# Batch 0's output matmuls regrouped inside cycles 6 to 8: one 64x64 run per cycle

## The chip, the cores and the metric

The kernel runs on one core of a Trainium2 chip. The metric is the device time of one execution in microseconds (us). Three runs of the kernel before gave 340.65, 340.74 and 341.85 us, median 340.74. A core has a matrix engine (TensorE, PE in the profile; its weight loads are PEld), a vector engine (DVE), an activation engine (ACT), GpSimd (POOL) and SyncE (SP). Here POOL issues the loads and SP issues the transposing DMAs and the stores. Each engine works through its own list of instructions in order and waits on semaphores that the others raise.

## The reference

`reference()` is sigmoid attention followed by an MLP-mixer block, on q, k, v of shape (8, 12, 448, 64):

```python
scores = np.matmul(q, k.transpose(0, 1, 3, 2)) / np.sqrt(64) - np.log(448)
attn_out = np.matmul(1.0 / (1.0 + np.exp(-scores)), v)          # (8, 12, 448, 64)
x = attn_out.transpose(0, 2, 1, 3).reshape(8, 448, 768)
h = np.maximum(x.transpose(0, 2, 1) @ w_tok1, 0.0) @ w_tok2       # tokens 448 -> 256 -> 448
u = x + h.transpose(0, 2, 1)
h2 = np.maximum(u @ w_ch1, 0.0) @ w_ch2                           # channels 768 -> 1536 -> 768
return u + h2
```

## The kernel before

The twelve heads of a batch are handled as three units of four heads, so there are 8 x 3 = 24 cycles, numbered c = 3b + u (b the batch, u the unit). A cycle has seven score steps. `qk(b, u, j)` (L187) makes a group of four 64x64 matmuls, which use the four quarters of the matrix engine at once and together stream 448 columns, and then a sigmoid on ACT (L194). I call four such matmuls a quad. The score results have two PSUM buffers, so a score step waits for the sigmoid of two steps before. `av` (L218) multiplies the attention with v, 28 matmuls or 7 quads a unit, and two DVE casts (L227) bring the result into the tile `xu`; `xtrans_dma` (L243, SP) transposes that by DMA. `tok_tail` and `tok1` (L277, L296) and `ytrans` (L316, L326) are the token mixing, two cycles behind. Once a batch has its three units, `ch1` makes the hidden tile `h2` from u and w_ch1, and `ch2` multiplies `h2` with w_ch2. From batch 1 on the first product runs in the function `sevens`, in seven instead of eight block products (L516), with sums of weights from `weight_sums` (L432), differences of tokens from `token_sums` (L459), and later sums of w_ch2 from `output_sums` (L746, twelve DVE instructions in groups of three, t1 to t4). For batch 0 it is plain.

The matrix engine is used in two ways: as 128x128 (ch1, ch2, token mixing, `sevens`) and as four 64x64 quarters (scores, av, the small `tok_tail`). A stretch of consecutive 64x64 work is called a 64x64 run here.

The order is written by hand (`tc.manual_schedule()`), and what is issued first on an engine runs first. The diff touches cycles 5 to 9, about 58 to 109 us of the profile:

- Cycle 5 ends with the output products of batch 0 for two (t, half) pairs, `pieces_ch2(0, by_half[:2])`. t counts tiles of 128 tokens, half the halves of the 768 channels. Each is 12 matmuls of 384 columns (L586) and three of 128 columns that add u (L597), and one DVE copy out (L616).
- Cycles 6, 7 and 8 spread the other four pairs and the last half tile (`ch2_last`, L893, L904) between the scores by shares (`work`). Each of these cycles thereby has three 64x64 runs: scores 0, 1, av and score 2; scores 3, 4 (with `tok_tail` in cycles 6 and 7); scores 5, 6 (with `tok_tail` in cycle 8). Every piece also takes a waiting DVE step along: `copies`, or `early`, the weight sums.
- The copies of cycles 7 and 8 are `through_dma(3, 0)`: three DVE relayouts of k (L129), the DMA transpose of k (L142, SP), three relayouts of q, the DMA transpose of q. The scores of cycle 9 read both.
- Cycle 8 ends with `utrans` (L339, L343: a DMA transpose of 24 blocks on SP), `token_sums`, then `sevens(1)`, which takes eight of the twelve `output_sums` along, and `gated_loads`: a POOL copy (L1136) waits for the transposed q of batch 3 and then v of batch 3 and k of batch 4 are loaded (L118).
- From cycle 9 on `steady` already has one 64x64 run a cycle. It uses `quads`, `two_jobs` and `split_steps`, which do a 128x128 product as quads. In a pair, two products share the quads, and after the first turn `turn_over` (L854, a DVE copy of one column) separates the turns, in which the two row halves swap their PSUM banks. The remaining `output_sums` run in cycles 9 and 10 (`more`), before VectorE adds the results of `ch2_seven` into the output (L843).

```python
def some(n):                       # the next n waiting copies
ORDER = "1ab 2a 2b 1c 6ab 5ab 2c 6c 5c 7ab 7c 3ab 4ab 3c 4c"   # sevens
more((0, 3)[u])                    # steady: output sums at the head of cycles 9, 10
```

Of the kernel before, what the change touches and what calls it, by code (L numbers as in the profile page):

```python
# [21 lines left out]
NJ = 7  # L22
# [1 line left out]
NU = 3  # L24
NS = 224
BY_GROUP = [0, 1, 6, 7, 2, 3, 8, 9, 4, 5, 10, 11]
OPENING_BANKS = "2013013013013021302130213021302131302121302130213020213012"


@with_exitstack  # L30
def kernel(
# [322 lines left out]
    def ut(b, db):  # L354
        return xu(b)[:, db % NU, db // NU, :]
# [306 lines left out]
        turns = [[lambda t=t, n=n: step(t, n) for n in range(n_quads)] for t in range(2)]  # L662
        return turns[0], turns[1], rest

    def split_steps(ps, n_cb, lhsT, rhs):

        def step(n):
            for r in range(2):
                part = slice(64 * r, 64 * r + 64)
                for m in (0, 64):  # L670
                    nc.tensor.matmul(  # L671
                        out=ps[r][m : m + 64, 0:DH],
                        lhsT=lhsT(part, n, m),
                        rhs=rhs(part, n, m),
                        start=(n == 0),
                        stop=(n == n_cb - 1),
                    )

        return [lambda n=n: step(n) for n in range(n_cb)]
# [475 lines left out]
    for c, cb in ((N_FIRST, 3), (N_FIRST + 1, 8)):  # L1155
        b, u = divmod(c, NU)
        before = divmod(c - 1, NU)
        ahead = divmod(c + 1, NU)
        copies = []

        def whole(cb):
            for d in range(0, NDB, 3):
                ch1(0, cb, d, d + 3)
                if copies:
                    copies.pop(0)()

# [46 lines left out]
    pending, copies = [], []  # L1213

    def some(n):
        for f in copies[:n]:
# [6 lines left out]
    def sevens(b, banks=(2, 3, 0, 1, 0)):  # L1223
        step = ch1_seven(b, banks)
        for at, (n, gs) in enumerate(SEVENS):
            step(n, gs)
            some((2, 0, 1, 1, 1, 1, 1, 1)[at] if at < 8 else 0)

    early = weight_sums()
    lane = [0]  # L1230
    for c in range(2 * NU, ONE_RUN):
        b, u = divmod(c, NU)
        before, ahead = divmod(c - 1, NU), divmod(c - 2, NU)


        if c == 2 * NU:
            first = c
            pending, shares = [*pieces_ch2(0, by_half[2:]), *pieces_last(0)], [10, 10, 10]
            total = sum(w for w, f in pending)
            spent = 0  # L1240

        def work(share):
            goal = 3 * sum(shares[: c - first]) + share * shares[c - first]
            done = 0
            while pending and spent + done < total * goal / 90:
                w, f = pending.pop(0)
                if len(pending) % 4 == 3:
                    lane[0] ^= 1
                at_bank[0] = 2 + lane[0]
                f()  # L1250
                done += w
                if copies:
                    copies.pop(0)()
                elif early:
                    early.pop(0)()
            return done
# [8 lines left out]
        if c == 2 * NU + 2:  # L1265
            copies += through_dma(3, 0)[NU + 1 :]
        spent += work(1)
        qk(b, u, 3)
        qk(b, u, 4)
# [4 lines left out]
        spent += work(2)  # L1274
        if c == 2 * NU + 2:
            utrans(b - 1)
            token_sums(b - 1)
            spent += work(3)
        qk(b, u, 5)
        qk(b, u, 6)  # L1280
        at_bank[0] = 0
        if u < 2:
            ytrans(*ahead)
        else:
            tok_tail(*ahead)
            tok1(*ahead, with_scores=True)
        if c == 2 * NU + 1:
            copies += through_dma(3, 0)[: NU + 1]
        if u < 2:
            spent += work(3)  # L1290
        if u == 2:
            assert not copies
# [7 lines left out]
    assert not copies and not pending and not early  # L1300

    def more(n):
        for f in extra[:n]:
# [11 lines left out]
    def steady(b, u):  # L1315
# [12 lines left out]
        if u < 2:  # L1328
            if u == 0:
                sides = [h2[lot][:, :, 128 * t : 128 * t + 128] for t in range(2)]  # L1330
                sevenfold[lot] = ch2_seven(
                    [(lot, 0), (lot, 1)], sides, X, X + 1, X + 1, at_end=False
                )
                sevenfold[lot].sums(0, 2)
            more((0, 3)[u])
            seven = sevenfold[lot]
            turn0, turn, turn1, end = two_jobs([seven.job(n) for n in ((1, 2), (7, 3))[u]])
            score(2)
            run(turn0, 6)
# [167 lines left out]
```

## Time and profile before

| what | value |
|---|---|
| median of three runs | 340.74 us |
| the profiled execution | 340.27 us |
| its span, first to last instruction | 338.5 us |
| PE busy | 332.2 us, 98% |
| DVE busy | 235.3 us, 70% |
| ACT busy | 212.7 us, 63% |
| mean granted clock of TensorE | 0.998 |

The profiled execution has 1.77 us around its span. In the timeline, a row has the start in us from the beginning of the span, the length in us, the engine, the source line, the operation, what it writes and reads, and how many consecutive instructions were merged into the row (x12). A row's length reaches to the end of the last instruction. Matmuls overlap, so the next row can start before this one's length is over, and the distance between two starts tells what a row took of the engine. SPq is the queue that SyncE issues DMAs from; such a row's length is the time of issuing, not of landing.

### The profile page before, as it was taken

How to read it: one execution, taken by the hardware profiler on the slowest of the kernel's cores; microseconds unless marked ns; L12 is line 12 of the kernel's file. 1: busy time of each engine (PE TensorE's matmuls, PEld its weight loads, DVE VectorE, ACT ScalarE, POOL GpSimd, SP SyncE). 2: the span in 40 equal slices, each digit the busy share in tenths (PEclk: the TensorE clock that was granted, in tenths of full speed). 3: DMA queues.
4: the chain of work that ended last, by engine and by line, in shares of the span. 5: the costliest groups of instructions: out<-in, count | busy, mean ns of one | idle time of the engine just before them, and what ended most of it. 6: DMA issues, size and time to landing. Idle time of an engine off the chain costs nothing.

```text
span 338.5 us, 10318 instructions
## 1 busy us (share of the span) xinstructions
PE 332.2 (98%) x4436; PEld 242.9 (72%) x4436; DVE 235.3 (70%) x486; ACT 212.7 (63%) x272; POOL 61.7 (18%) x108
## 2 busy tenths in 40 slices
PE   8999999999999999999999999999999999999994
PEld 5655556555896679767896679766896679769852
DVE  2376466678998874877668774877768653976882
ACT  4996845388747885678647885678657895314200
POOL 8985380050031002020032001110010000000000
PEclk9999999999999999999999999999999999999999
DMA  8999999999999899989998899988993393028006
GB/s 128 162 160 202 207 178 203 175 175 234 186 179 194 158 171 203 182 125 179 186 190 133 152 151 215 201 123 163 195 179 65 67 171 85 2 56 186 4 13 196
DMA packets 103422, 51.91 MB, mean 153 GB/s; under 512 B 75473, under 2 KB 100305, under 8 KB 103377
## 3 DMA queue, kind: packets, MB, share of 16 engines
q1 hardware_dynamic: 77648, 28.84, 47.0%
q0 software_dynamic: 25264, 21.50, 42.4%
q10 hardware_dynamic: 464, 0.92, 1.0%
q8 instruction: 34, 0.56, 0.6%
q14 instruction: 12, 0.09, 0.1%
HBM read 43.45 MB, written 11.01 MB: 161 GB/s over the span
## 4 chain that ended last, share of the span: by engine, by line
PE 81%; DMA 11%; POOL 5%; DVE 1%; issue 1%; ACT 0%; ACTq 0%; POOLq 0%
PE c_ab L516 14%; PE c L816 10%; PE c_c L516 8%; PE qk L187 8%; PE xa L218 7%; PE c L863 6%; DMA raw_k<-in_k_dram 5%; PE tk L296 4%; PE yt L316 4%; PE c L586 4%; PE c L387 4%; DMA raw_v<-in_v_dram 3%; PE c L671 3%; DMA c<-in_moe_w_ch_dram 3%; PE c L652 2%; POOL raw_q L118 2%
## 5 line engine op out<-in xcount | busy, mean ns | idle before, releaser
L194 ACT ACTIVATE att<-qk,att_bias 128x896 f16<-128x896 f32 x168 | 155.9, 1012 | 37.8 <-PE qk L187 36.7
L187 PE MATMUL qk<-tr_q,tr_k 64*64 64x448 f16 x672 | 60.8, 357 | 0.3 <-DVE tr_k L179 0.2
L516 PEld LDWEIGHTS <-c 128*128 128x128 f16 x504 | 48.4, 98 | 1.1 <-issue 0.3
L218 PE MATMUL xa<-att,raw_v 64*64 64x448 f16 x644 | 40.6, 349 | 0.0
L187 PEld LDWEIGHTS <-tr_k 64*64 64x64 f16 x672 | 25.3, 104 | 18.7 <-issue 11.5
L516 PEld LDWEIGHTS <-sum 128*128 128x128 f16 x378 | 36.3, 98 | 0.0
L227 DVE CAST xu<-xa 128x448 f16<-128x448 f32 x40 | 23.1, 619 | 18.3 <-PE xa L218 17.9
L537 ACT ACTIVATE pt_ab<-c_ab 128x896 f32<-128x896 f32 x21 | 19.2, 917 | 20.6 <-PE c_ab L516 20.6
L218 PEld LDWEIGHTS <-raw_v 64*64 64x64 f16 x672 | 21.9, 107 | 8.2 <-issue 0.4
L863 PE MATMUL c<-c,h 64*64 64x384 f16 x360 | 24.6, 323 | 0.0
L1136 POOL COPY gate<-tr_q 128x2 f16<-128x2 f16 x6 | 1.1, 184 | 121.9 <-DMA tr_q<-rel_q 121.9
L326 DVE TENSOR_TENSOR xu<-xu,yt 128x448 f16<-128x448 f16 x38 | 21.8, 615 | 0.0
L539 ACT ACTIVATE h<-c_ab 128x896 f16<-128x896 f32 x7 | 6.4, 917 | 24.4 <-PE c_ab L516 24.4
L296 PE MATMUL tk<-xn,w 128*128 128x256 f16 x156 | 21.2, 274 | 0.1
L546 DVE TENSOR_TENSOR h<-pt_ab,c_ab 128x896 f16<-128x896 f32 x14 | 15.2, 1083 | 8.6 <-PE c_ab L516 8.6
L546 DVE TENSOR_TENSOR h<-pt_c,c_c 128x448 f16<-128x448 f32 x21 | 12.9, 616 | 11.7 <-PE c_c L516 11.6
L310 ACT ACTIVATE h<-tk 128x256 f16<-128x256 f32 x42 | 14.2, 405 | 9.9 <-PE tk L296 9.9
L316 PE MATMUL yt<-w,h 128*128 128x448 f16 x88 | 20.3, 353 | 0.0
L843 DVE TENSOR_TENSOR o<-un,c 128x384 f32<-128x384 f16 x32 | 17.4, 551 | 4.0 <-PE c L816 4.0
L816 PEld LDWEIGHTS <-hid 128*128 128x128 f16 x132 | 12.9, 98 | 8.0
L516 PE MATMUL c_ab<-diffs,c 128*128 128x224 f16 x168 | 18.4, 259 | 0.0
L118 POOL DMA_DIRECT2D raw_k<-in_k_dram x26 | 16.8, 661 | 8.0 <-DMA c<-in_moe_w_ch_dram 5.6
(132 smaller groups left out, 574.4 us busy)
## 6 DMA issues: line engine op xcount, KB each, us to landing
out_dram<-o SPq DMA_DIRECT2D x41, 192.0 KB, 3.3
c<-in_moe_w_ch_dram POOLq DMA_DIRECT2D x3, 1152.0 KB, 11.6
raw_k<-in_k_dram POOLq DMA_DIRECT2D x10, 336.0 KB, 6.6
raw_q<-in_q_dram POOLq DMA_DIRECT2D x10, 336.0 KB, 5.6
raw_v<-in_v_dram POOLq DMA_DIRECT2D x10, 336.0 KB, 8.2
raw_q<-in_q_dram POOLq DMA_DIRECT2D x16, 112.0 KB, 5.9
raw_k<-in_k_dram POOLq DMA_DIRECT2D x16, 112.0 KB, 6.9
out_dram<-o SPq DMA_DIRECT2D x15, 96.0 KB, 2.4
```

Source lines behind the costliest of these rows:

```text
L118: nc.gpsimd.dma_start(out=dst.rearrange("p u hi j e -> p (u hi) (j e)"), in_=heads.rearrange("h (p j) e -> p h (j e)", j=NJ),)
L187: nc.tensor.matmul(out=ps[64 * g : 64 * g + 64, hi, 0:S], lhsT=tr[b, "k"][64 * hi : 64 * hi + 64, u, j, 64 * g : 64 * g + 64], rhs=tr[b, " ...
L194: nc.scalar.activation(out=att[b, u, j][:, :, :], in_=ps[:, :, 0:S], func=SIGMOID, bias=bias_t[:, :], scale=att_scale,)
L218: nc.tensor.matmul(out=ps[g][64 * hi : 64 * hi + 64, 0:S], lhsT=raw[b, "v"][64 * g : 64 * g + 64, u, hi, j, :], rhs=att[b, u, j][64 * g : ...
L227: nc.vector.tensor_copy(out=xu(b)[:, u, g, 0:S], in_=ps[g][:, 0:S])
L296: nc.tensor.matmul(out=ps[tcb], lhsT=w1[rows, t, cols], rhs=xn[b, u][rows, :, t, :], start=(t == 0 and not with_scores), stop=(t == (2 if ...
L316: nc.tensor.matmul(out=ps[:, 0:S], lhsT=h1[b, u][:, tcb, g, :], rhs=w2[:, tcb, :, :], start=(tcb == 0), stop=(tcb == 1),)
L326: nc.vector.tensor_tensor(out=x, in0=x, in1=ps[:, 0:S], op=ADD)
L516: nc.tensor.matmul(out=ps[:, g, p, :], lhsT=weights[n][:, d, 128 * cb : 128 * cb + 128], rhs=moving[n][:, d, :], start=(n in (1, 5, 2) and ...
L546: nc.vector.tensor_tensor(out=shaped(dst), in0=shaped(parts[gs, which]), in1=ps, op=ADD)
L816: nc.tensor.matmul(out=ps[:, 0:DH], lhsT=self.weights[n][:, k, :], rhs=self.moving[n][:, k, :], start=(n in (1, 2, 5) and k == 0), stop=(k ...
L863: nc.tensor.matmul(out=ps[m : m + 64, 0:DH], lhsT=lhsT(n)[part, m : m + 64], rhs=rhs(n)[part, :], start=(opens and turn == 0 and n == 0), ...
```

## The change

1. Cycle 5 does one (t, half) pair instead of two.
2. Cycles 6 and 7 do two pairs each, `first_pair`: eight of the twelve 128-row blocks as quads in the cycle's one 64x64 run, between scores, in two turns of eight; the last four blocks and the adding of u as plain 128x128 matmuls (`rest`) behind the token mixing. Scores 3 to 6 all lie in that run. `av` moves behind the first turn; the early weight sums are issued three and three in each of the two cycles.
3. Cycle 8 does the last half tile first, wholly in quads (`first_last`, two partial sums, added on DVE), and the pair (2, 1) with four blocks in quads and eight plain (`first_split`: one partial sum is copied out on DVE ahead of `token_sums`, the other added at the end).
4. The order on SP and DVE in cycle 8 changes with it: the relayouts of k and its transpose now all stand at the head of cycle 8, right behind `ytrans` of cycle 7; the three of q and q's DMA transpose come behind `rest`, two relayouts before `sevens` and the third and the transpose after its first step. `utrans` and the stores of tile (0, 2) now stand ahead of q's transpose on SP, and the stores of the last half tile too.
5. `sevens(1)` takes six `output_sums` along instead of eight; in cycle 9, `more(3)` in place of `more(1)` runs three.

```diff
-    def split_steps(ps, n_cb, lhsT, rhs):
+    def split_steps(ps, n_cb, lhsT, rhs, open_ended=()):
...
-                        stop=(n == n_cb - 1),
+                        stop=(n == n_cb - 1 and r not in open_ended),
+                        skip_group_check=bool(open_ended),
...
-            for w, f in pieces_ch2(0, by_half[:2]):
+            for w, f in pieces_ch2(0, by_half[:1]):
...
+    def plain_rest(t, half, ps, n_quads):
+        for n in range(n_quads, NCB):
+            nc.tensor.matmul(out=ps[:, 0:DH], lhsT=h2[0][:, BY_GROUP[n], 128 * t : 128 * t + 128],
...
+        add_u(t, half, ps)
+    def first_pair(rows, n_quads):
...
+        ps = [bank([128, 512], FP32, f"c2_0_{t}_{half}") for t, half in rows]
+        turn_bank[0] = ps[1]
...
+        def rest():
+            for p, (t, half) in enumerate(rows):
+                plain_rest(t, half, ps[p], n_quads)
+                ch2_out(0, t, half, ps[p])
...
+    def first_split(t, half, n_quads):
...
+        def copy_out():
+            nc.vector.tensor_copy(out=o, in_=ps[1][:, 0:DH])
+        def rest():
+            plain_rest(t, half, ps[0], n_quads)
+            nc.vector.tensor_tensor(out=o, in0=o, in1=ps[0][:, 0:DH], op=ADD)
+            store(0, t)
...
+    def first_last():
...
+        def end():
+            for n in range(NU):
+                for r in range(2):
+                    part = slice(64 * r, 64 * r + 64)
+                    for m in (0, 64):
+                        nc.tensor.matmul(
+                            out=ps[r][m : m + 64, 128 * n + 64 * r : 128 * n + 64 * r + 64],
+                            lhsT=ut(0, NU * (m // 64) + n)[part, 384:448],
+                            rhs=ident[part, 64 * r : 64 * r + 64],
...
+            nc.vector.tensor_copy(out=o[:, :], in_=ps[0][:, 0:DH])
+            nc.vector.tensor_tensor(out=o[:, :], in0=o[:, :], in1=ps[1][:, 0:DH], op=ADD)
...
         some(len(copies))
         qk(b, u, 0)
         qk(b, u, 1)
-        at_bank[0] = 0
-        av(*before)
-        xtrans_dma(*before)
-        qk(b, u, 2)
...
         if u < 2:
+            turn0, turn1, rest = first_pair(by_half[1 + 2 * u : 3 + 2 * u], 8)
+            run(turn0, 7)
+            sums_early(3)
+            qk(b, u, 2)
+            run(turn0, 1)
+            turn_over(turn_bank[0])
+            sums_early(3)
+            av(*before, 0, 4)
+            qk(b, u, 3)
+            av(*before, 4, NJ)
+            xtrans_dma(*before)
+            run(turn1, 1)
+            qk(b, u, 4)
+            run(turn1, 4)
+            qk(b, u, 5)
+            run(turn1, 3)
+            tok_tail(*ahead)
+            qk(b, u, 6)
+            tok1(*ahead, with_scores=True)
+            rest()
+            ytrans(*ahead)
+            if u == 1:
+                copies += through_dma(3, 0)[: NU + 1]
+        else:
+            steps, end = first_last()
+            run(steps, 7)
+            qk(b, u, 2)
+            run(steps, NCB)
+            qk(b, u, 3)
+            end()
+            av(*before, 0, 4)
+            qk(b, u, 4)
+            steps, copy_out, rest = first_split(2, 1, 4)
+            av(*before, 4, NJ)
+            xtrans_dma(*before)
+            run(steps, 1)
+            utrans(b - 1)
+            qk(b, u, 5)
+            run(steps, 3)
+            copy_out()
+            token_sums(b - 1)
+            qk(b, u, 6)
             tok_tail(*ahead)
             tok1(*ahead, with_scores=True)
+            rest()
+            copies += through_dma(3, 0)[NU + 1 :]
+            some(2)
             extra = output_sums()
-            copies += extra[:8]
-            del extra[:8]
+            copies += extra[:6]
+            del extra[:6]
             sevens(b - 1)
...
                 seven.sums(2, 4)
-                more(1)
+                more(3)
```

More of the change, by code (lines that the diff above doesn't have):

```diff
@@ L1211 @@
             gated_loads(b)
-    pending, copies = [], []
+    copies = []
     def some(n):
@@ L1227, in sevens, with add_u @@
             some((2, 0, 1, 1, 1, 1, 1, 1)[at] if at < 8 else 0)
+    def add_u(t, half, ps):
+        for n in range(NU):
+            nc.tensor.matmul(
+                out=ps[:, 128 * n : 128 * n + 128],
+                lhsT=ut(0, NU * half + n)[:, 128 * t : 128 * t + 128],
+                rhs=ident[:, :],
+                start=False,
+                stop=(n == NU - 1),
+                skip_group_check=True,
+            )
+    def plain_rest(t, half, ps, n_quads):
+        for n in range(n_quads, NCB):
+            nc.tensor.matmul(
+                out=ps[:, 0:DH],
+                lhsT=h2[0][:, BY_GROUP[n], 128 * t : 128 * t + 128],
+                rhs=c2[:, BY_GROUP[n], DH * half : DH * half + DH],
+                start=False,
+                stop=False,
+                skip_group_check=True,
+            )
+        add_u(t, half, ps)
@@ new lines, in first_pair, with step @@
+    def first_pair(rows, n_quads):
+        for t, half in rows:
+            if (0, t) not in outs:
+                out_tile(0, t)
+        ps = [bank([128, 512], FP32, f"c2_0_{t}_{half}") for t, half in rows]
+        turn_bank[0] = ps[1]
+        def step(turn, n):
+            quads(
+                ps,
+                DH,
+                turn,
+                lambda p, part, m: h2[0][
+                    part, BY_GROUP[n], 128 * rows[p][0] + m : 128 * rows[p][0] + m + 64
+                ],
+                lambda p, part: c2[
+                    part, BY_GROUP[n], DH * rows[p][1] : DH * rows[p][1] + DH
+                ],
+                n == 0,
+                False,
+                True,
+            )
+        def rest():
+            for p, (t, half) in enumerate(rows):
+                plain_rest(t, half, ps[p], n_quads)
+                ch2_out(0, t, half, ps[p])
+        turns = [[lambda t=t, n=n: step(t, n) for n in range(n_quads)] for t in range(2)]
+        return turns[0], turns[1], rest
@@ new lines, in first_split @@
+    def first_split(t, half, n_quads):
+        ps = [bank([128, 512], FP32, f"c2_0_{t}_{half}_{r}") for r in range(2)]
+        cols = slice(DH * half, DH * half + DH)
+        steps = split_steps(
+            ps,
+            n_quads,
+            lambda part, n, m: h2[0][
+                part, BY_GROUP[n], 128 * t + m : 128 * t + m + 64
+            ],
+            lambda part, n, m: c2[part, BY_GROUP[n], cols],
+            open_ended=(0,),
+        )
+        o = outs[0, t][:, cols]
+        def copy_out():
[4 more added lines that the diff above has]
+            store(0, t)
+        return steps, copy_out, rest
@@ new lines, in first_last @@
+    def first_last():
+        ps = [bank([128, 512], FP32, f"c2_0_3_{r}") for r in range(2)]
+        steps = split_steps(
+            ps,
+            NCB,
+            lambda part, n, m: h2[0][part, BY_GROUP[n], 384:448],
+            lambda part, n, m: c2[
+                part, BY_GROUP[n], DH * (m // 64) : DH * (m // 64) + DH
+            ],
+            open_ended=(0, 1),
+        )
+        def end():
+            for n in range(NU):
+                for r in range(2):
+                    part = slice(64 * r, 64 * r + 64)
+                    for m in (0, 64):
+                        nc.tensor.matmul(
+                            out=ps[r][m : m + 64, 128 * n + 64 * r : 128 * n + 64 * r + 64],
+                            lhsT=ut(0, NU * (m // 64) + n)[part, 384:448],
+                            rhs=ident[part, 64 * r : 64 * r + 64],
+                            start=False,
+                            stop=(n == NU - 1),
+                            skip_group_check=True,
+                        )
+            o = last_tile(0)
+            nc.vector.tensor_copy(out=o[:, :], in_=ps[0][:, 0:DH])
+            nc.vector.tensor_tensor(out=o[:, :], in0=o[:, :], in1=ps[1][:, 0:DH], op=ADD)
+            for g in range(2):
+                nc.sync.dma_start(
+                    out=orow[0, NJ - 1][:, DH * g : DH * g + DH],
+                    in_=o[64 * g : 64 * g + 64, :],
+                )
+        return steps, end
@@ L1233, with run, sums_early @@
         before, ahead = divmod(c - 1, NU), divmod(c - 2, NU)
[L1236 to L1249, printed above, removed]
-                f()
[L1251 to L1256, printed above, removed]
+        def run(steps, n):
+            for f in steps[:n]:
+                f()
+            del steps[:n]
+        def sums_early(n):
+            for f in early[:n]:
+                f()
+            del early[:n]
         some(len(copies))
@@ L1273 @@
             tok1(*ahead, with_scores=True)
[L1274 to L1292, printed above, removed]
+            rest()
+            copies += through_dma(3, 0)[NU + 1 :]
+            some(2)
             extra = output_sums()
-            copies += extra[:8]
-            del extra[:8]
+            copies += extra[:6]
+            del extra[:6]
             sevens(b - 1)
@@ L1299 @@
             gated_loads(b)
-    assert not copies and not pending and not early
+    assert not copies and not early
     def more(n):
```

15 lines of the change are left out of this document (8 added, 7 removed).

## The prediction

> **What bounds the kernel now.** I read the page's busy shares first, then the stages the change touches by windows, then the engines' timelines there.
>
> ```profile
> PE 332.2 (98%) x4436; PEld 242.9 (72%) x4436; DVE 235.3 (70%) x486; ACT 212.7 (63%) x272; POOL 61.7 (18%) x108
> 80.21:87.77 7.56, 7.45 (x107) 4.54 (x107) 7.01 (x16) 5.82 (x8) 0.00 (x0) 1.00 1.14 261
> ```
>
> The columns of a window are its length, then busy time of PE, PEld, DVE, ACT and POOL. PE is busy throughout at full clock, so only the time its own work takes, and waits newly put before it, can move the end. DVE, 7.01 of 7.56 us in cycle 8, is nearly full there. The PE timeline of cycles 6 to 9:
>
> ```profile
> 60.78 0.33 PE L597 MATMUL c<-ident,xu_first 128*128 128x128 f16 x3
> 60.95 2.11 PE L586 MATMUL c<-c,h 128*128 128x384 f16 x12
> 62.90 0.33 PE L597 MATMUL c<-ident,xu_first 128*128 128x128 f16 x3
> 63.16 0.57 PE L187 MATMUL qk<-tr_q,tr_k 64*64 64x448 f16 x8
> 63.56 1.50 PE L218 MATMUL xa<-att,raw_v 64*64 64x448 f16 x28
> 64.88 0.36 PE L187 MATMUL qk<-tr_q,tr_k 64*64 64x448 f16 x4
> 65.18 1.64 PE L586 MATMUL c<-c,h 128*128 128x384 f16 x9
> ...
> 85.95 0.33 PE L904 MATMUL c<-ident,xu_first 128*64 128x128 f16 x6
> 86.21 0.57 PE L187 MATMUL qk<-tr_q,tr_k 64*64 64x448 f16 x8
> 86.61 0.28 PE L277 MATMUL tk<-xn,w 64*64 64x256 f16 x4
> 86.83 0.83 PE L296 MATMUL tk<-xn,w 128*128 128x256 f16 x6
> 87.77 1.31 PE L516 MATMUL c_ab<-xu,c 128*128 128x224 f16 x12
> ...
> 100.71 0.57 PE L187 MATMUL qk<-tr_q,tr_k 64*64 64x448 f16 x8
> ```
>
> Every x8 row of L187 opens a 64x64 run; there are nine from 63.16 to 86.21. What one run costs, by distances of starts: twelve 384-column matmuls take 62.90 - 60.95 = 1.95 us, 0.1625 each; three L597 take 60.95 - 60.78 = 0.17; a 448-column quad takes (64.88 - 63.56) / 7 = 0.189. Into the run: 62.90 + 0.17 = 63.07, but the scores start at 63.16, 0.09 late. Its first two quads take 0.40 instead of 0.38, 0.02 more. Out of it: 64.88 + 0.19 = 65.07, but L586 starts at 65.18, 0.11 late. A run costs 0.22 us beside its work.
>
> **The change part by part.**
>
> *Fewer runs.* Cycles 6 to 8 have three runs each; afterwards one. Six go: 6 x 0.22 = 1.32 us gained, on PE's path. Nothing else of PE's work changes: the same five blocks of 12 x 0.1625 us stand before yt in cycle 7, and a quad of a split product covers 128x128 weights like one matmul.
>
> *The last half tile.* Six L904 took 86.21 - 85.95 - 0.09 = 0.17; twelve 64-column matmuls in three quads replace them. By columns they take 3 x 64 x 0.1625 / 384 = 0.08; were each serial at an L597's 0.17 / 3, 0.68. Like the quads above they run four at a time, so I take 0.17, no difference, and keep -0.1 and +0.5 for the range. The Trainium skill ("TensorEngine Tiling (Array Packing)", section "Instruction Overhead") states that each matmul has about 60 cycles of overhead, so that few columns are no faster than 60; 64 columns are above that, and by it the sum would have 0.08 here. No row here has so short a quad.
>
> *The wait ahead of `sevens`.* The six of L296 end their turn at 86.83 + 6 x 0.11 = 87.49 (0.11 is (0.83 - 0.28) / 5, a last matmul of the same columns lasting 0.28), and L516 starts at 87.77: 0.28 us lost.
>
> ```profile
> 86.71 1.90 ACT L194 ACTIVATE att<-qk,att_bias 128x896 f16<-128x896 f32 x2 [0.84 <-PE qk L187]
> 82.14 1.16 DVE L227 CAST xu<-xa 128x448 f16<-128x448 f32 x2 [0.44 <-PE xa L218]
> ```
>
> It waits for the first sigmoid (86.71 + about 1.0), whose score buffer it takes. Now 8 x 0.1625 + 0.17 = 1.47 us of `rest` stand between: 0.28 gained.
>
> *Token mixing in cycle 8, a new wait.* The second bank of `tok_tail` needs av's second cast. Before, casts ended at 83.30 and it came at 86.61. Now four quads of 0.1625 and two of scores (1.03) stand behind av's last quad (0.19): PE arrives 1.22 after that quad's start, while the quad ends at 0.35, casts take 1.16 and handing over about 0.1: 1.60. Cost 0.38. In cycles 6 and 7 eight quads and two score steps (1.68) stand there and cover it.
>
> *`turn_over` and early sums.* The copy waits for turn 0; behind it on DVE are sums and casts; PE's turn 1 waits for it. av and a score step, 8 x 0.189 = 1.51, cover it. Sums are ready-made work for DVE and issued six per cycle; 0. Without cover the six would cost up to 2.8 us.
>
> *Three output sums in cycle 9 instead of one.*
>
> ```profile
> 104.00 1.16 DVE L227 CAST xu<-xa 128x448 f16<-128x448 f32 x2 [0.93 <-PE xa L218]
> ...
> 107.29 0.55 DVE L746 TENSOR_TENSOR hsum_b<-c 128x768 f16<-128x768 f16 x1
> 107.75 1.05 DVE L843 TENSOR_TENSOR o<-un,c 128x384 f32<-128x384 f16 x2
> 108.72 1.15 DVE L326 TENSOR_TENSOR xu<-xu,yt 128x448 f16<-128x448 f16 x2
> 109.78 1.49 DVE L746 TENSOR_TENSOR hsum_b<-c,hsum_a 128x768 f16<-128x768 f16 x3
> ```
> ```profile
> 109.30 0.32 PE L863 MATMUL c<-c,h 64*64 64x384 f16 x1
> ...
> 110.28 0.36 PE L218 MATMUL xa<-att,raw_v 64*64 64x448 f16 x4
> ```
>
> DVE is without a pause from 104.00 on. Two more sums are 2 x (1.49 - 0.55) / 2 = 0.94. The L843 pair moves to 108.69 to 109.70 (from its start, 0.46 apart); the next pair of products reuses that bank at 109.30, so PE waits 0.40, with handing over 0.45. The L326 adds end at 110.77, when av wants their banks at 110.28 + 0.45: 0.1 more. Cost 0.55. What was 0.94 of DVE in `sevens` hid nothing PE waited for.
>
> *q's transpose for batch 3, past six items on SP.*
>
> ```profile
> 81.72 4.09 SPq L142 DMA_TRANSPOSE tr_k<-rel_k  x1
> 85.99 1.23 SPq L243 DMA_TRANSPOSE xn<-xu  x1
> 87.28 2.15 SPq L623 DMA_DIRECT2D out_dram<-o  x2
> 89.53 4.37 SPq L142 DMA_TRANSPOSE tr_q<-rel_q  x1
> 93.99 3.75 SPq L343 DMA_TRANSPOSE un<-xu  x1
> 97.84 1.18 SPq L925 DMA_DIRECT2D out_dram<-o  x2
> ```
> ```profile
> 95.96 0.18 POOL L1136 COPY gate<-tr_q 128x2 f16<-128x2 f16 x1 [22.14 <-DMA tr_q<-rel_q]
> ```
>
> SP issues with hardly a pause from 81.72 to 99.02, 17.30 us. tr_q landed by 95.96, 2.06 after its issue ended, 4.75 before the scores of cycle 9 at 100.71. Now it is the last of these same items. The list starts with tr_k, behind yt of cycle 7, which comes four runs (0.88) earlier: 80.84. It ends at 98.14, and tr_q lands at 100.2. PE arrives at 100.71 - 1.32 - 0.28 + 0.38 = 99.49: it waits 0.7. The other end, from rows of a later batch:
>
> ```profile
> 122.16 5.07 SPq L343 DMA_TRANSPOSE un<-xu  x1
> 127.34 3.29 SPq L142 DMA_TRANSPOSE tr_q<-rel_q  x1
> ```
>
> The first pair of stores at 1.18, as the last, instead of 2.15, and un and tr_q at 130.63 - 122.16 = 8.47 instead of 8.21, make it 16.6: landed at 99.5, no wait. I take 0.5, nearer the rows of this place. The relayouts of q on DVE end at about 88.1 (80.84 and the 7.3 us of VectorE's work worked out under the rivals); SP gets there at 98.14 - 4.37 = 93.8. Behind tr_q stand POOL's gate and the loads of v. Those were issued by 97.85 and landed after 8.4 at most:
>
> ```profile
> 96.47 1.38 POOL L118 DMA_DIRECT2D raw_v<-in_v_dram  x2 [0.33 <-issue]
> DMA to landing us min/median/max: 7.6/8.0/8.4
> ```
>
> So the second lands 97.85 - 1.38 / 2 + 8.4 - 95.96 = 9.6 after tr_q, while av asks 110.28 - 100.71 + 0.45 = 10.0 after scores that themselves wait for tr_q. Covered by 0.4; 0.
>
> *Sum.* -1.32 - 0.28 + 0.38 + 0.55 + 0.5 = -0.17 us. The profiled execution's 340.27 becomes 340.10; the median lay 0.47 above it, so 340.57, said as **340.6 us**.
>
> **The rivals.**
>
> *The queue and DVE keep up.* If SP takes 16.6 us, and DVE's sums slip into pauses, -1.32 - 0.28 + 0.38 = -1.22: 339.5. For it: those SP rows. Against: DVE has no pause from 104.00 to 109.87.
>
> *Slower: tr_q lands late.* un landed 8.1 us after issue, 4.3 after its issue ended, with loads in flight. If tr_q as last of the queue lags as much, it lands at 102.4, PE waits 3.0 instead of 0.5, and v with it: +2.3, 343.1. It decides when tr_q lands after 101.8. Against: those loads now wait for tr_q itself, and it lagged 2.06 without them.
>
> ```profile
> DMA to landing us min/median/max: 8.1/8.1/8.1
> ```
>
> *VectorE becomes the bound in cycle 8.* From 80.84 to 86.5 it has, by rows of the same kind, the last tile's copy and add (1.1), casts (1.16), edge copies (0.4), copy-out and add (1.0), token sums (about 2.0) and q's relayouts (three of 0.6): about 7.3 us in 5.7. 1.6 spill into `sevens`, whose third group takes its bank only 2.3 us after VectorE freed it:
>
> ```profile
> 90.06 0.62 DVE L546 TENSOR_TENSOR h<-pt_ab,c_a 128x448 f16<-128x448 f32 x1 [0.26 <-ACT pt_ab L537]
> 92.96 0.74 PE L516 MATMUL c_c<-xu,c 128*128 128x224 f16 x6
> ```
>
> It decides above 2.3; at 3.0, +0.7: 341.3. The Trainium skill ("TensorEngine Tiling (Array Packing)", section "PSUM Bottleneck") speaks for it: tiling speeds up TensorE but not the copies out of PSUM, which can become the bound and should go to ScalarE too; the change adds copies on VectorE alone.
>
> *The runs cost the same in another place*, if turns or bank changes inside a run stall PE as a switch does: no gain of 1.32, +1.15: 341.9. Against: quads and scores alternate from 102.28 on at 0.19 (L187 at 102.28, L218 at 102.46).
>
> ```profile
> 102.28 0.36 PE L187 MATMUL qk<-tr_q,tr_k 64*64 64x448 f16 x4
> 102.46 0.93 PE L218 MATMUL xa<-att,raw_v 64*64 64x448 f16 x16
> ```
>
> **How the numbers follow.** Forecast 0.60, queue and DVE keep up 0.14, tr_q late 0.12, VectorE bound 0.10, runs cost the same 0.04. The range 339.5 to 342.2 goes from the second case to between the third's onset and its price, and holds the ends of the small terms (-0.1, +0.5). Within 0.5%, about what a measurement of this kernel can tell from none, is 339.04 to 342.44: faster 0.03, same 0.85 and slower 0.12, nearly all the late transpose.
>
> **What would show it.** Three x8 rows of L187 in cycles 6 to 8, starting about 61, 69.7 and 78.3; L516 following L586 without a gap; PE idle ahead of L277 in cycle 8 (0.4), ahead of cycle 9's first scores, released by DMA tr_q (0.5, start near 100.0), and in cycle 10 ahead of the quads, released by DVE's o (0.45). All later cycles keep their length. The prediction is wrong if PE waits in cycles 6 or 7, for v in cycle 10, or more than 2 us for tr_q.

## The result and the profile after

The changed kernel takes 345.93 us (median of eight executions, 344.14 to 353.99), the kernel before, beside it on the same chip, 340.69 (340.41 to 341.92). The ratio is 1.0124 [1.0102, 1.0145], slower by 1.2%; forecast were 340.6 us and no change. Three of the eight executions took 351 to 354 us and are left out of the ratio, and the profiled one, 350.97, is one of them; so a second execution of the same kernel, 344.30 us, is read beside it below (`e1_after`).

The page of the changed kernel, its busy times and the granted clock in 40 slices of 8.7 us:

```profile
PE 334.3 (96%) x4574; PEld 247.7 (71%) x4574; DVE 236.1 (68%) x489; ACT 212.6 (61%) x272; POOL 61.7 (18%) x108
PEclk9999999999999879999999999999999999999999
```

TensorE is no longer busy throughout, and its clock falls in the two slices from 113.5 to 131 us. Its timeline:

```profile
61.46 0.57 PE L187 MATMUL qk<-tr_q,tr_k 64*64 64x448 f16 x8
...
70.13 0.57 PE L187 MATMUL qk<-tr_q,tr_k 64*64 64x448 f16 x8
...
78.81 0.57 PE L187 MATMUL qk<-tr_q,tr_k 64*64 64x448 f16 x8
...
84.28 0.61 PE L277 MATMUL tk<-xn,w 64*64 64x256 f16 x4
...
86.79 0.33 PE L1232 MATMUL c<-ident,xu_first 128*128 128x128 f16 x3
86.96 1.31 PE L516 MATMUL c_ab<-xu,c 128*128 128x224 f16 x12
...
99.03 0.92 PE L316 MATMUL yt<-w,h 128*128 128x448 f16 x4
101.60 0.57 PE L187 MATMUL qk<-tr_q,tr_k 64*64 64x448 f16 x8 [1.65 <-DMA tr_q<-rel_q]
...
121.76 0.43 PE L277 MATMUL tk<-xn,w 64*64 64x256 f16 x4 [6.81 <-DMA xn<-xu]
```

Up to 99.03 this is the change as forecast: three runs of scores, one per cycle, no pause ahead of L516, L277 stretched from 0.28 to 0.61 by the wait for the cast. Then two waits on DMA: 1.65 us for q's transpose, 6.81 us for the transpose `xn` that token mixing of cycle 10 reads. SP's queue in the same execution:

```profile
81.38 3.93 SPq L142 DMA_TRANSPOSE tr_k<-rel_k  x1
85.41 1.19 SPq L1341 DMA_DIRECT2D out_dram<-o  x2
86.70 2.09 SPq L243 DMA_TRANSPOSE xn<-xu  x1
88.88 3.64 SPq L343 DMA_TRANSPOSE un<-xu  x1
92.61 1.19 SPq L623 DMA_DIRECT2D out_dram<-o  x2
93.90 4.17 SPq L142 DMA_TRANSPOSE tr_q<-rel_q  x1
106.33 9.82 SPq L243 DMA_TRANSPOSE xn<-xu  x2
```

POOL's gate and the loads behind it, and two pieces of the chain that ended last (start, length, what):

```profile
101.59 0.47 POOL L1137 COPY gate<-tr_q 128x2 f16<-128x2 f16 x1 [29.27 <-DMA tr_q<-rel_q]
102.10 1.32 POOL L118 DMA_DIRECT2D raw_v<-in_v_dram  x2
```

```profile
93.90 7.57 DMA tr_q<-rel_q
...
106.33 15.38 DMA xn<-xu
```

tr_q lands at 93.90 + 7.57 = 101.47, the loads start 102.10 - 96.47 = 5.6 us later than before, and `xn`, issued at 106.33, lands only 15.4 us later. In the kernel before it was issued at 105.44, landed 4.6 us later, and nothing waited for it:

```profile
105.44 9.42 SPq L243 DMA_TRANSPOSE xn<-xu  x2
```

### The profile page after: what moved, and what is told of

Same layout as the page of the kernel before. It is cut to its first block, busy times and chain, and to the rows that moved or that the text cites. A ratio compares the mean times of both kernels' runs of the same rounds, so it can differ in the third digit from the quotient of the medians.

```text
span 349.2 us, 10595 instructions
## 1 busy us (share of the span) xinstructions
PE 334.3 (96%) x4574; PEld 247.7 (71%) x4574; DVE 236.1 (68%) x489; ACT 212.6 (61%) x272; POOL 61.7 (18%) x108
## 4 chain that ended last, share of the span: by engine, by line
PE 75%; DMA 16%; POOL 6%; DVE 1%; issue 1%; DVEq 0%; POOLq 0%
PE c_ab L516 13%; PE c L817 10%; PE c_c L516 8%; PE qk L187 7%; PE xa L218 6%; PE c L864 5%; PE c L387 5%; DMA xn<-xu 4%; PE tk L296 4%; PE yt L316 4%; PE c L671 4%; DMA raw_v<-in_v_dram 3%; DMA c<-in_moe_w_ch_dram 3%; DMA raw_q<-in_q_dram 3%; PE c L652 2%; DMA tr_q<-rel_q 2%
## 5 line engine op out<-in xcount | busy, mean ns | idle before, releaser
L187 PE MATMUL qk<-tr_q,tr_k 64*64 64x448 f16 x672 | 62.8, 356 | 1.9 <-DMA tr_q<-rel_q 1.6
L516 PEld LDWEIGHTS <-c 128*128 128x128 f16 x504 | 48.3, 98 | 0.8
L218 PE MATMUL xa<-att,raw_v 64*64 64x448 f16 x644 | 41.6, 349 | 0.0
L187 PEld LDWEIGHTS <-tr_k 64*64 64x64 f16 x672 | 26.5, 104 | 19.9 <-issue 12.6
L516 PEld LDWEIGHTS <-sum 128*128 128x128 f16 x378 | 36.3, 98 | 0.0
L227 DVE CAST xu<-xa 128x448 f16<-128x448 f32 x40 | 23.1, 619 | 15.8 <-PE xa L218 15.5
L218 PEld LDWEIGHTS <-raw_v 64*64 64x64 f16 x672 | 23.0, 107 | 7.6 <-issue 0.4
L864 PE MATMUL c<-c,h 64*64 64x384 f16 x360 | 24.6, 323 | 0.1
L387 PE MATMUL c<-c,h 64*64 64x384 f16 x408 | 23.8, 323 | 0.0
L296 PE MATMUL tk<-xn,w 128*128 128x256 f16 x156 | 21.8, 279 | 0.1
L387 PEld LDWEIGHTS <-h 64*64 64x64 f16 x408 | 16.4, 106 | 3.4 <-issue 1.1
```

The lines of the kernel that those rows point to most:

```text
L187: nc.tensor.matmul(out=ps[64 * g : 64 * g + 64, hi, 0:S], lhsT=tr[b, "k"][64 * hi : 64 * hi + 64, u, j, 64 * g : 64 * g + 64], rhs=tr[b, " ...
L218: nc.tensor.matmul(out=ps[g][64 * hi : 64 * hi + 64, 0:S], lhsT=raw[b, "v"][64 * g : 64 * g + 64, u, hi, j, :], rhs=att[b, u, j][64 * g : ...
L227: nc.vector.tensor_copy(out=xu(b)[:, u, g, 0:S], in_=ps[g][:, 0:S])
L296: nc.tensor.matmul(out=ps[tcb], lhsT=w1[rows, t, cols], rhs=xn[b, u][rows, :, t, :], start=(t == 0 and not with_scores), stop=(t == (2 if ...
L387: nc.tensor.matmul(out=ps[p][m : m + 64, 0:n], lhsT=lhsT(p, part, m), rhs=rhs(p, part), start=(first and turn == 0), stop=(last and turn = ...
L516: nc.tensor.matmul(out=ps[:, g, p, :], lhsT=weights[n][:, d, 128 * cb : 128 * cb + 128], rhs=moving[n][:, d, :], start=(n in (1, 5, 2) and ...
```

## The experiments

The kernel before runs beside each of them; its medians there are 340.8 to 341.2. Theories: Q, q's transpose is late and TensorE waits for it; L, POOL's loads, late with it, hold back `xn`; R, the regrouped matmuls cost more than they save.

### The changed kernel again

> The changed kernel once more, for a profile and for its spread. Theory L (late loads): q's transpose of batch 3 lands at about 101.5 us in place of 96; POOL's gate then starts the loads of v, k (four of 336 KB) at about 102, so that they are in flight when cycle 9's transpose of xn is issued at about 106.3; that transpose lands after them, and cycle 10's token mixing waits for it by 2 to 7 us, more where q's loads (issued at 108) are caught too. 344 to 351 us. Rival R (the regrouped order itself): PE waits of several us stand in cycles 6 to 8 as well. Rival Q (q's transpose alone): the only new wait over 0.6 us is that of cycle 9's first scores, about 1.6 us, and the time would be 341.5 to 342.

344.29 us (four executions, 343.85 to 351.23), ratio 1.009 [1.0069, 1.0112]. TensorE's timeline, and then a window behind the wait (columns as in the prediction; the last three are granted clock, DMA share, GB/s):

```profile
59.19 2.11 PE L586 MATMUL c<-c,h 128*128 128x384 f16 x12
...
86.89 1.31 PE L516 MATMUL c_ab<-xu,c 128*128 128x224 f16 x12
...
98.97 0.92 PE L316 MATMUL yt<-w,h 128*128 128x448 f16 x4
102.46 0.96 PE L187 MATMUL qk<-tr_q,tr_k 64*64 64x448 f16 x8 [2.57 <-DMA tr_q<-rel_q]
103.18 2.16 PE L864 MATMUL c<-c,h 64*64 64x384 f16 x24
105.10 0.57 PE L218 MATMUL xa<-att,raw_v 64*64 64x448 f16 x4
...
108.36 0.37 PE L277 MATMUL tk<-xn,w 64*64 64x256 f16 x4
```

```profile
102.46:105.10 2.64, 2.64 (x33) 1.69 (x37) 0.00 (x0) 1.90 (x2) 2.15 (x4) 0.50 0.26 23
```

SP's queue and POOL's gate:

```profile
81.32 5.67 SPq L142 DMA_TRANSPOSE tr_k<-rel_k  x1
...
95.68 4.00 SPq L142 DMA_TRANSPOSE tr_q<-rel_q  x1
```

```profile
102.45 0.18 POOL L1137 COPY gate<-tr_q 128x2 f16<-128x2 f16 x1 [29.14 <-DMA tr_q<-rel_q]
```

The same stretch in the kernel before, behind its first scores at 100.71:

```profile
101.11 1.15 PE L863 MATMUL c<-c,h 64*64 64x384 f16 x24
102.09 0.36 PE L218 MATMUL xa<-att,raw_v 64*64 64x448 f16 x4
...
105.14 0.36 PE L277 MATMUL tk<-xn,w 64*64 64x256 f16 x4
```

TensorE waits 2.57 us for tr_q, and then runs at a granted clock of 0.50: the eight score matmuls take 103.18 - 102.46 = 0.72 instead of 0.40, the 24 matmuls of six quads 1.92 instead of 0.98. From the first scores to L277 it is 108.36 - 102.46 = 5.90 us, before 105.14 - 100.71 = 4.43: 1.47 more. No wait for `xn` in this execution. So here the late q alone, with the clock behind the wait, makes the loss. That is the pattern of Q, but not its 341.5 to 342, which had no clock in it. Of the better executions only this one was profiled.

### q's relayouts and transpose early, the rest of the change kept

```diff
             xtrans_dma(*before)
+            copies += through_dma(3, 0)[NU + 1 :]
+            some(4)
...
             rest()
-            copies += through_dma(3, 0)[NU + 1 :]
-            some(2)
```

> The changed kernel with q's three relayouts and its transpose put back ahead of un's on SyncE and VectorE (right behind xn's transpose of cycle 8); everything else as changed. Theory L and rival Q: tr_q lands by about 96, no wait for it, the loads start by 97, xn's transpose of cycle 9 lands within 5 us and nothing waits: 340.7 - 1.6 + 0.4 + 0.55 = 340.0, within 339.4 to 340.6. Rival R: stays at 344 or more.

340.29 us (339.93 to 342.51), ratio 0.9996 [0.9977, 1.0016]. No wait for tr_q or `xn` is left in the list of waits. The regrouping is innocent (R falls), and the whole loss hangs on the place of q's relayouts and transpose in the order. Two rows show what still keeps a gain from coming:

```profile
88.48 0.74 PE L516 MATMUL c_b<-xu,c 128*128 128x224 f16 x6
89.25 0.73 PE L516 MATMUL c_c<-xu,c 128*128 128x224 f16 x6
...
108.06 0.57 PE L187 MATMUL qk<-tr_q,tr_k 64*64 64x448 f16 x8
108.46 0.34 PE L864 MATMUL c<-hsum_b,hid 64*64 64x384 f16 x2
108.92 0.35 PE L864 MATMUL c<-c,h 64*64 64x384 f16 x2
```

c_c comes 0.77 behind c_b instead of 0.57: VectorE now does q's relayouts ahead of the token sums, so its add of the output (L1306) runs from 88.65 to 89.20 instead of from 87.20 as in the changed kernel, and c_c starts right behind it; and in cycle 10 the second half of the quads starts at 108.92 instead of 108.46, behind the three output sums.

### Only q late, in the kernel before

```diff
-        if c == 2 * NU + 2:
-            copies += through_dma(3, 0)[NU + 1 :]
...
+            copies += through_dma(3, 0)[NU + 1 :]
+            some(4)
             sevens(b - 1)
```

> The kernel before with q's relayouts and transpose put behind un's transpose and the stores of the last half tile, and nothing regrouped. SyncE's list then ends with tr_q at about 99, landing at about 101. Theory L: the loads start at about 101 to 102 and xn's transpose of cycle 9 (105.4) lands after them: a wait in cycle 10 of 2 to 7 us, 342.5 to 348. Rival R: no such wait, 340.7 to 341.3. Rival Q: only a wait of at most 0.6 ahead of cycle 9, 340.7 to 341.3.

341.07 us, ratio 0.9995 [0.9983, 1.0008]: eight of eleven executions at 340.3 to 341.3, three at 350.7 to 352.8. One of the three was profiled; in it tr_q opened the gate at 102.58, and the list of waits has

```profile
PE tk L277 <- DMA xn<-xu: 7.7, 1, 7.7
```

as in the profiled execution of the changed kernel. There TensorE also waited 1.50 us ahead of cycle 9's first scores (L187 at 102.59, right behind the gate). L's 342.5 to 348 came in none of the eleven: eight lie at or just below the 340.7 to 341.3 of Q and R, and three above L's range. Without the regrouping TensorE arrives 1.25 us later (100.71 against 99.46), which may be why eight of eleven lose nothing; none of the eight was profiled, so this is not shown.

### Only the loads late, in the kernel before

```diff
-            out=gate[:, :], in_=tr[b + 1, "q"][:, NU - 1, NJ - 1, 126:128]
+            out=gate[:, :],
+            in_=h2[1][:, NCB - 1, 0:2] if b == 2 else tr[b + 1, "q"][:, NU - 1, NJ - 1, 126:128],
```

> The kernel before with one thing changed: POOL's gate of cycle 8 reads the last written part of h2 of batch 1 (ready at about 101) instead of q's transpose (96), so that the loads of v and k start 5 us later while every transpose and every other engine's order stays. Theory L: xn's transpose of cycle 9 is held back by the loads, cycle 10 waits 2 to 7 us: 342.5 to 348, with tr_q in time. Rivals R and Q: 340.7, within 0.5, as long as v is in time.

345.97 us (four executions, 345.17 to 350.25), ratio 1.0169 [1.0104, 1.0234].

```profile
100.94 1.32 POOL L118 DMA_DIRECT2D raw_v<-in_v_dram  x2 [0.33 <-PE qk L187]
```

```profile
116.53 0.30 PE L277 MATMUL tk<-xn,w 64*64 64x256 f16 x4 [3.34 <-DMA xn<-xu]
```

q's transpose is in time here, and no matmul was moved; the loads alone, 100.94 - 96.47 = 4.5 us later, make `xn` late by 3.34 us at L277. This is L by itself.

### The loads early, in the changed kernel

```diff
-            out=gate[:, :], in_=tr[b + 1, "q"][:, NU - 1, NJ - 1, 126:128]
+            out=gate[:, :],
+            in_=tr[b + 1, "k" if b == 2 else "q"][:, NU - 1, NJ - 1, 126:128],
```

> The changed kernel, but POOL's gate of this one batch reads k's transpose instead of q's, so that the loads of v and k no longer wait for the late transpose of q. Theory L (transposes on SP's queue hardly move while POOL's loads are in flight): the loads now start near 88 to 90 us and fall on un and on q's transpose, tr_q lands well after 102.3, PE waits more than 2.6 us for it, xn of cycle 10 is no longer held back; 345 or more. Rival Q (tr_q is late only because six items stand before it on SP, each with its own length): tr_q lands at 102.3 as before, PE waits 2.6, nothing waits for xn, and the time is 344.3 with no run near 350.

352.73 us, ratio 1.0333 [1.0311, 1.0355].

```profile
90.52 1.32 POOL L118 DMA_DIRECT2D raw_v<-in_v_dram  x2 [0.25 <-issue]
```

```profile
95.51 11.28 SPq L142 DMA_TRANSPOSE tr_q<-rel_q  x1
```

```profile
109.05 0.96 PE L187 MATMUL qk<-tr_q,tr_k 64*64 64x448 f16 x8 [9.06 <-DMA tr_q<-rel_q]
```

Beside the loads even the issuing of tr_q takes 11.28 us instead of 4.0, and TensorE waits 9.06. The same transfers in another order: whichever transpose falls on the loads is the late one. L's numbers came, and the 344.3 of rival Q did not.

### Work in the wait for tr_q

```diff
+            if b == NU and u == 0:
+                fill = pp.tile([128, 2, 512], FP32, tag="qk", bufs=2, name="fill")
+                for n in range(14):
+                    nc.tensor.matmul(
+                        out=fill[:, n % 2, 0:DH],
+                        lhsT=h2[1][:, n % NCB, 0:128],
+                        rhs=c2[:, n % NCB, 0:DH],
...
             score(2)
```

> The changed kernel with 14 products of 384 columns, whose result nobody reads, ahead of the first scores of cycle 9: 2.3 us of work in the time in which PE waits for tr_q. Theory W (after the wait PE is granted half its clock for some 3 us, which costs 1.3 to 1.5 us, because it had been idle): no slow scores after the wait, PE's clock stays near 1.0, and the time is about 1.4 us below that of the changed kernel, 342.9 against 344.3, though PE has more work. Rival: the scores after the wait are slow for what else runs then (the loads, ScalarE's and POOL's work): they stay slow, the time is 344.3.

> The changed kernel with 14 unread products ahead of cycle 9's first scores, once more, because the times of its first run spread over 7 us. Theory W: wherever tr_q is all that PE waits for, the time is that of the changed kernel (344.3, or 1.009 of the kernel before) less the 1.4 us of half clock: 342.9, 1.006 of the kernel before. Rival: the half clock has to be paid at the next wait anyway, or xn of cycle 10 takes up what is saved, as the first run's median of 346.3 would have it: 344.3 or more.

```profile
103.02 2.44 PE L1471 MATMUL fill<-c,h 128*128 128x384 f16 x14
105.73 0.57 PE L187 MATMUL qk<-tr_q,tr_k 64*64 64x448 f16 x8 [0.27 <-DMA tr_q<-rel_q]
106.11 1.17 PE L864 MATMUL c<-c,h 64*64 64x384 f16 x24
107.08 0.39 PE L218 MATMUL xa<-att,raw_v 64*64 64x448 f16 x4
```

```profile
105.70:106.70 1.00, 0.97 (x24) 0.85 (x28) 0.00 (x0) 0.54 (x1) 0.66 (x2) 1.00 0.00 0
```

These rows are of the first series. The same wait, filled with work, and the clock stays at 1.00: scores 0.38, quads 0.97, with the loads and ScalarE's work behind it as before. So idling, and not what else runs then, is what halves the clock. The total did not follow cleanly. First 346.33 us (343.22 to 350.75), ratio 1.0137 [1.0104, 1.017], then 348.36 (343.02 to 355.54), ratio 1.0105 [1.0055, 1.0156]; of thirteen executions three took 343.0 to 343.2, which is 0.6 to 1.3 below the three better ones of the kernel without the filling (343.85 to 344.30), and the others 346 to 355.5. In the worst one, profiled in the second series, `xn` of cycle 10 was waited for:

```profile
125.08 0.43 PE L277 MATMUL tk<-xn,w 64*64 64x256 f16 x4 [6.15 <-DMA xn<-xu]
```

So W is right about the clock, and its 342.9 was nearly met in three executions of thirteen; no saving in the median is shown. The profiles have a reading for the rest. In both filled ones `xn` of cycle 10 is issued 4.23 us after the first of POOL's loads (110.46 - 106.23 and 110.31 - 106.08), as in the 350.97 execution of the changed kernel (106.33 - 102.10), with only q late (4.24) and with only the loads late (4.20). In these five `xn` lands 10.8 to 15.8 us after its issue. In the 344.30 execution it is issued 5.71 us after the loads (108.67 - 102.96) and lands 6.8 us later, in time. The 1.48 us between the two distances are the half clock's 1.47. By this reading the slow clock itself kept `xn` off the loads in that execution, and the filling takes this away. No run moved `xn` alone, and the three at 343.0 to 343.2, which were not profiled, show that such an execution can still get through.

### The output sums

Eight and one sums, as in the kernel before, and seven and two, both with q early:

```diff
-            copies += extra[:6]
-            del extra[:6]
+            copies += extra[:8]
+            del extra[:8]
...
-                more(3)
+                more(1)
```

> The kernel with q's relayouts and transpose ahead of un, and in it eight output sums in the seven products and one in cycle 9, as before the change, instead of six and three. If the three sums in cycle 9 cost PE 0.46 us ahead of the products of cycle 10, as the profile shows, and VectorE has room for two more in the seven products: 339.85, against 340.3 for the same kernel with three. If the two sums only make the first matrix products wait in cycle 8 instead (a pause of 0.7 us is there for 1.0 us of sums): 340.1 to 340.3.

> The same with seven sums in the seven products and two in cycle 9. One sum of 0.47 us fits the pause of 0.7 us on VectorE in cycle 8, and in cycle 9 the adds of o come 0.47 us earlier, so PE's wait of 0.46 us goes: 339.85. If it is not the number of sums that makes the adds late: 340.3.

Eight and one: 340.58 us (339.60 to 345.02), ratio 0.9987 [0.9968, 1.0007]. Seven and two: 341.80 (339.63 to 345.58), ratio 1.0014 [0.9982, 1.0045]. The wait in cycle 10 is gone with both, and the best executions are 0.3 below the 339.93 of three sums in cycle 9, though the forecast 339.85 came in neither median, and neither ratio is clear of 1. Both spread more than the kernel before did on that chip (340.26 to 341.76, one 344.29). The profiled execution of eight and one, 341.95 us, shows one such delay, in cycle 8:

```profile
86.69 0.30 PE L277 MATMUL tk<-xn,w 64*64 64x256 f16 x4 [1.61 <-DMA xn<-xu]
```

Token mixing came there at 86.61 in the kernel before, and comes at 84.3 after the change. That gave theory S: the change used up the slack of this transpose, hence the spread.

### More slack for cycle 8's transpose

Ten quads of the second half of tile 2 ahead of token mixing instead of four (first diff), or all its plain products (second), both with q early and eight sums in the seven products:

```diff
-            steps, copy_out, rest = first_split(2, 1, 4)
+            steps, copy_out, rest = first_split(2, 1, 10)
...
             run(steps, 3)
-            copy_out()
             token_sums(b - 1)
             qk(b, u, 6)
+            run(steps, 6)
+            copy_out()
```

```diff
+            rest()
             at_bank[0] = 0
             tok_tail(*ahead)
             tok1(*ahead, with_scores=True)
-            rest()
```

> The kernel with q's transpose ahead of un and eight output sums in the seven products, and in it ten quads of the second half of tile 2 in cycle 8's 64x64 run instead of four (the copy behind them, six plain products fewer behind token mixing): token mixing of cycle 8 is asked 6 x 0.1625 = 0.98 us later. Theory S (the change took 2.3 us of slack from the transpose xn that cycle 8 reads, which lands between 81.8 and 87.8 us from run to run, while its readers come at 84.3 instead of 86.6): fewer and shorter waits for xn, the runs above 341 become rarer, and the 0.25 us in which token mixing waits for VectorE's cast goes too: best runs 339.4, median 339.9. Rival (the spread has nothing to do with this transpose): the spread of 339.6 to 345 stays as it was.

> The same kernel with four quads, but the plain products of that half tile ahead of token mixing instead of behind it: token mixing comes 1.47 us later, at the price of a fourth 64x64 run (0.22) and of the pause before the seven products (up to 0.28). Theory S: nearly no run waits for xn, the runs lie as close together as those of the kernel before (340.3 to 341.7), with the best ones at 339.9 to 340.1. Rival: best runs at 340.1 and the same tail up to 345.

> The kernel with q's transpose ahead of un and eight sums in the seven products once more, beside the two others on the same chip: best runs 339.6, median 340.5, single runs up to 345 in which token mixing of cycle 8 waits for xn.

Ten quads: 340.47 us (339.77 to 348.11), ratio 1.0001 [0.9984, 1.0017]. Plain products first: 340.43 (339.65 to 349.69), ratio 0.9990 [0.9973, 1.0008]. Unchanged: 339.88 (339.58 to 339.97, seven executions), ratio 0.9975 [0.9965, 0.9986]. More slack did not narrow the spread, and the one without it had none this time: so the runs do not bear out S as the explanation of the spread, though the wait of 1.61 us was real. No long execution of these three series was profiled, so which transfer was late in them is not known, and what makes one series quiet and the next not stays open. The kernel with q early and eight sums in the seven products is the best version seen: 0.9975 in one series and 0.9987, an interval that reaches past 1, in the other.

```profile
107.88 0.57 PE L187 MATMUL qk<-tr_q,tr_k 64*64 64x448 f16 x8
108.28 0.32 PE L864 MATMUL c<-hsum_b,hid 64*64 64x384 f16 x1
108.28 0.32 PE L864 MATMUL c<-c,h 64*64 64x384 f16 x1
```

In its profile both halves of cycle 10's quads start together, 0.40 behind the scores.

## Why the prediction was wrong

The terms, measured in the 344.30 us execution against the 340.27 of the kernel before. Its cycle 6 starts 59.19 - 58.83 = 0.36 us later (L586 stands at 58.83 before), which is no part of the change.

| term | forecast | measured | from |
|---|---|---|---|
| six runs fewer, no pause before L516, wait for the cast | -1.22 | -1.24 | L516 at 86.89 instead of 87.77, less 0.36 |
| TensorE waits for tr_q | +0.5 | +2.6 | L187 at 102.46 |
| clock after that wait | not thought of | +1.5 | 5.90 - 4.43 |
| three sums in cycle 9 | +0.55 | +0.4 | L277 to L277 of cycles 9 and 10: 116.94 - 108.36 = 8.58, before 113.33 - 105.14 = 8.19 |
| loads behind the gate | 0 | 0 here, 2.3 to 7.7 where `xn` waits | L277 of cycle 10 |

With the 0.36 the table gives +3.6; the last product starts 337.26 - 333.61 = 3.65 us later, and the remaining 0.4 of 344.30 - 340.27 = 4.03 lies behind it, in the last stores.

*Right.* All of TensorE's own side. It reached cycle 9 at 98.97 + 0.85 - 0.36 = 99.46; forecast 99.49. The cast's wait is 0.3 (L277 to L296 take 0.54 instead of 0.22), forecast 0.38. The twelve 64-column matmuls in quads took about 0.1 us (in the 350.97 execution L1329 from 81.55, `av` behind it from 81.64), so here the Trainium skill ("TensorEngine Tiling (Array Packing)", section "Instruction Overhead") was nearer with its 0.08 than my 0.17. VectorE did not become the bound; only with q's relayouts earlier does its spill delay a product of `sevens`, by 0.2, and it is the first c_c, at 89.25, not the one at 92.96 that the rival named. The quads behind the sums started 0.45 late in this execution too, as forecast; the 0.1 behind them did not come.

*The step that failed* is "q's transpose for batch 3, past six items on SP", in three places.

First its size. I had tr_q land between 99.5 and 100.2, and took 0.5. It landed at 101.5 in one profile and just before 102.45 in the other. The list's start was right (81.38 and 81.32 less 0.4, forecast 80.84). Issuing took 16.7 us in the one and 18.4 in the other, forecast 16.6 to 17.3; and POOL's gate opened 3.5 (101.59 - 98.07) and 2.8 us (102.45 - 99.68) after the issue's end, where I had taken 2.06, read the same way, from the old place. Both ends of my range were rows of other moments: the length of a transpose's issue and its lag change from place to place and from run to run, and what sets them no run here shows. The kernel before had longer lags on record: its transposes of L142 issued at 155, 232 and 242 us landed 3.4 to 3.5 us after their issue ended. The rival "tr_q lands late" had this case, landing at 102.4, and its condition of 101.8. Its argument against itself, that the lag would be short because the loads wait for tr_q, did not hold: the lag was long without them. So 0.12 was too little for it. The top of the range, 342.2, does not fit its own description either: tr_q at 101.8 means a wait of 2.3 instead of 0.5, which gives 342.4.

Second, what a wait does to TensorE. That rival was priced at the wait alone, 343.1. The clock adds 1.5: in the 344.30 execution the granted clock is 0.50 until 105.50, about 3 us after work resumes. The Trainium skill ("TensorE: Matmul & The Clock Gate", section "HAM oscillation — how this bites in real kernels") warns of idle gaps over about 3.4 us; here 2.57 us were enough in one execution, and 1.65 in another were not. The prediction has no term for the clock at all.

Third, what hangs on tr_q. I followed the loads behind POOL's gate to their reader, found v covered by 0.4 and put 0, which was right for v. I did not ask which transfers the later loads would then meet. `xn` of cycle 10 is issued at the end of cycle 9; before, two of the four loads had landed within 0.1 us of its issue, and in the 350.97 execution none had. The fourth experiment shows that late loads alone cost 1.7%, and the fifth that the reverse order starves tr_q instead. In the 344.30 execution of the changed kernel this did not strike, and by the reading of the filled runs that was luck in part, since the half clock had put `xn` 1.47 us later; in the 350.97 execution it cost 6.81 us, and half clock behind it. With a wait of more than 2 us for tr_q the prediction had named its own failure, but not the transpose behind the loads, and that all later cycles would keep their length was wrong wherever `xn` waits.

## What to carry to other kernels

A DMA that is moved back on its queue moves everything that is gated on its landing: follow those transfers too, and ask of each later transfer what it will now overlap. Where a transfer has thin cover, its lag in the old place is a poor price for the new one; take the worst lag of its kind in the profile. A new wait on TensorE can cost more than its length: here one of 2.57 us cost 1.47 us more in clock, and one of 1.65 us nothing more.

## What the runs showed of the hardware

Transposes issued from SP progress slowly while POOL's loads are in flight: tr_q took 11.28 us to issue instead of 4.0, and `xn` 15.4 us to land instead of the 4.6 before, when half of the loads were through. The Trainium skill ("DMA: Bandwidth & Descriptors", section "Queues, rings and completion order") says that each DMA engine takes packets from its queues in turn. For tr_q the trace agrees with sharing, in unequal parts: from 96 to 98 us of the run with early loads POOL's queue moved 0.27 MB and SP's 0.04 MB, where SP's alone had moved 0.38 MB from 92 to 94 us. For `xn` sharing is not the whole of it: from 112 to 116 us of the 350.97 execution both queues together moved 80 GB/s, against 175 from 104 to 112 us, and the four other profiles in which `xn` waits have such a stretch too (62 to 84 GB/s over 2 us or more). What makes the DMA engines slow in it stays open.

TensorE's granted clock fell to 0.50 within the wait of 2.57 us and stayed there for about 3 us of work, and matmuls whose result nobody reads kept it at 1.00 in the same place. It also fell just behind waits of 3.34 us (only the loads late) and 2.27 us (the first filled profile), and not at waits of 1.50, 1.61 and 1.65 us; but a wait of 1.76 us early in the second filled profile was followed by a fall at 25.30, so these runs give no sharp limit.
